# Attention's transposes and value products taken two units at a time, from the fifth query tile on

## The chip, the cores and the metric

The kernel runs on one core of one Trainium2 chip. The metric is the device time of one execution, in microseconds (us), of which the median over several runs is taken. TensorE does the matmuls and the transposes, VectorE and ScalarE read their results out of PSUM, GpSimd scales and splits what lies in SBUF, and SyncE's queue issues the DMAs.

## What is computed

Three stages in a row: causal attention with a decay, a mixture of eight experts whose gates are normalised over rows and columns in turn, and a second feed-forward layer. The change touches the first one only:

```python
B, H, S, D = 2, 8, 576, 64
scores = q @ k.T / sqrt(D) + cum[:, None] - cum[None, :]     # cum: running sum of log f
scores = where(causal, -1e9, scores)
attn = exp(scores - max(scores)); attn /= attn.sum() + 1e-9
out = attn @ v                                               # becomes x of the experts
```

## The kernel before

Attention takes ten query tiles: batch 0 has rows 0, 128, 256, 384 (128 rows each) and 512 (64 rows), batch 1 has row 0 (64 rows) and then 64, 192, 320, 448 (128 rows each). The program counts them `ti` = 0 to 9, so "from the fifth on" is `ti >= 4`. Each tile is four **units** of two heads; unit `pi` = 4 ti + `st`, 40 in all. `nk` is the number of keys that a unit looks at; in the tiles 4 to 9 it is 576, 64, 256, 384, 512 and 576. A 64-row tile puts its two heads into one set of 128 rows.

The schedule is written by hand: every engine executes its instructions in the order in which the program emits them. The main loop has two steps per unit, `s` = 2 pi + a. A step emits, in this order:

- `expo` (line 487): ScalarE's exponential for the step before, with the row sums.
- `normalize` (line 497), where a = 1, for unit pi-1: two small VectorE instructions make 1/sum, and GpSimd multiplies the two heads with it.
- `scores` (line 452; `scores_two`, line 402, for 64-row tiles): two fp32r matmuls per head (L467, L468, or L415) into a PSUM bank of the pool `ps_s`, which has two banks, and VectorE's masked maximum (L480 or L421), which frees the bank. With `nk` = 576 a head takes both banks. The result `p` has three buffers.
- `fill`: one piece (three matmuls, L621 or L640) of expert 0's work, in two lots of 28 pieces, one ready early in the fourth tile, the other once the seventh tile has been attended; in between there are steps without a piece.
- where a = 1: `attend` (line 558) for unit pi-3: the products with v (L567), in column halves of TensorE's array, into one PSUM bank per tile, copied to `xh` and `xl` after the tile's last unit.
- where a = 1: `transposes` (line 516; `transposes_two`, line 436) for unit pi-2: it turns `p` by TensorE (L531 in 64-row halves of the array; L543, L448, L554 with the whole array or a part of its columns) into banks of the pool `ps_t` (three banks), and ScalarE or VectorE copies them to `pT` (two buffers), whichever has the smaller load by the planner's own tally (`evac`, L308 and L312).
- parts of the next tile's preparation: `qs` and `ks` in the steps (st 0, a 0) and (0, 1) split the raw queries and keys into two parts (`hl`, two buffers) on ScalarE, VectorE and GpSimd; `qt_(0)`, `kt_(0)`, `qt_(1)`, `kt_(1)` (`trans`, line 356) in (1, 0), (1, 1), (2, 0) and (2, 1) turn four heads each by TensorE (L360, into `ps_t`), copy them to `qa` or `kt`, and send a DMA that duplicates them to `qb` or `kb`. SyncE's queue also gets the loads of later tiles, of v and of the running sums there.

After the loop follow the gates' last part, the leftover pieces, and the experts.

Of the kernel before, what the change touches and what calls it, by code (L numbers as in the profile page):

```python
# [9 lines left out]
FR = mybir.dt.float32r  # L10
# [6 lines left out]
B, H, S, D = 2, 8, 576, 64  # L17
# [66 lines left out]
def attention_moe_kernel(  # L84
# [44 lines left out]
    with ExitStack() as actx:  # L129
# [8 lines left out]
        ps_s = actx.enter_context(tc.tile_pool(name="ps_s", bufs=2, space=PSUM))  # L138
        ps_t = actx.enter_context(tc.tile_pool(name="ps_t", bufs=3, space=PSUM))
# [193 lines left out]
        def prep(kind, b, i, slots):  # L333

            s0, n = QT[b][i] if kind == "q" else KTL[i]
            st = {}

            def split(half=None):
                if not half:
                    st["raw"] = raws.pop((kind, b, s0))  # L340
                    if (b, i) == (0, 1):
                        o = 1024 * (kind == "k")
                        st["hl"] = big[:, o:o + 1024].rearrange("p (h z d) -> p h z d", z=2, d=D)
                    else:
                        st["hl"] = hlp.tile([128, H, 2, D], FR, tag="hl", name="hl")
                raw, hl = st["raw"], st["hl"]
                hs = slice(0, H) if half is None else slice(4 * half, 4 * half + 4)
                z = 0 if kind == "q" else 1
                hi, lo = hl[:n, hs, z, :], hl[:n, hs, 1 - z, :]
                if half is None:  # L350
                    split2(raw[:n], hi, lo)
                else:
                    nc.scalar.copy(out=hi, in_=raw[:n, hs])
                    nc.vector.tensor_tensor(out=lo, in0=raw[:n, hs], in1=f(hi), op=ALU.subtract)

            def trans(g, early=False):
                hl = st["hl"]
                pt = ps_t.tile([128, 4, 128], FR, tag="pt", name="pt")
                for u in range(4):
                    nc.tensor.transpose(  # L360
                        out=pt[:, u, :n],
                        in_=hl[:n, 4 * g + u].rearrange("p a d -> p (a d)"),
                        identity=idr[:n, :n],
                    )
                hs = slice(4 * g, 4 * g + 4)
                pv = f(pt[:, :, :n])
                if kind == "q":
                    a_, b_ = qa[slots[g]], qb[slots[g]]
                    if n == 64:
                        evac(quads(a_)[:, :, 0:4:3], pv.rearrange("p (u z) t -> p u z t", z=2), 4 * n, 0.125)  # L370
                    else:
                        evac(a_[:, :, :n], pv, 4 * n, 0.125)
                    if early:
                        evac(b_[0:64, :, :n], pv[0:64], 4 * n, 0.125)
                    else:
                        duplicate(b_[0:64], a_[0:64])
                        if g:
                            cum_q(b, i, g, slots[g])
                else:
                    o = kbase[b] + s0  # L380
                    evac(kt[:, hs, o:o + n], pv, 4 * n)
                    if early:
                        evac(kb[0:64, hs, o:o + n], pv[64:128], 4 * n)
                    else:
                        duplicate(kb[0:64, hs, o:o + n], kt[64:128, hs, o:o + n])

            return split, trans
# [170 lines left out]
        def attend(u):  # L558
            n, nk, h, b, pT = u["n"], u["nk"], u["h"], u["b"], u["pT"]
            if h == 0:  # L560
                u["tile"]["x"] = ps_x.tile([128, 4, 128], F32, tag="x", name="x")
            x = u["tile"]["x"]
            nblk = (nk + 127) // 128
            for j in range(nblk):
                w = 128 if j == 4 else min(128, nk - 128 * j)
                for a in range(2):
                    nc.tensor.matmul(  # L567
                        out=x[64 * a:64 * a + 64, h // 2, :n], lhsT=vts[b, j][:w, h + a, :],
                        rhs=pT[:w, 128 * j + 64 * a:128 * j + 64 * a + 64] if n == 64 else pT[:w, a, j * n:(j + 1) * n],
                        start=j == 0, stop=j == nblk - 1,  # L570
                    )
            if h == H - 2:
                c, t0 = divmod(b * S + u["s0"], CH)
                nc.scalar.copy(out=xh[c][:, :, t0:t0 + n], in_=x[:, :, :n])
                nc.vector.tensor_tensor(
                    out=xl[c][:, :, t0:t0 + n], in0=x[:, :, :n], in1=f(xh[c][:, :, t0:t0 + n]), op=ALU.subtract
                )
                spent("act", 90 + 3.4 * n)
                spent("dve", 90 + 4.2 * n)
# [80 lines left out]
        units = []  # L660
# [14 lines left out]
        def make_preps(ti):  # L675
            b, i = tiles[ti]
            slots = [(2 * ti) % 3, (2 * ti + 1) % 3]
            return prep("q", b, i, slots), prep("k", b, i, slots)
# [20 lines left out]
        wtasks = [lambda i=i: wsplit(i) for i in range(8)]  # L699
        gates, logits, ready = [], [], []  # L700
        nu = len(units)
        for s in range(2 * nu + 8):
            pi, a = divmod(s, 2)
            ti, st = divmod(pi, 4)
            live = pi < nu
            prepping = live and ti + 1 < len(tiles)
            if prepping and st == 0 and a == 0:
                (qs, qt_), (ks, kt_) = make_preps(ti + 1)
            if 1 <= s <= 2 * nu:
                expo(units[(s - 1) // 2], (s - 1) % 2)  # L710
            if a and 1 <= pi <= nu:
                normalize(units[pi - 1])
            if live:
                scores(units[pi], a)
            if s < 16:
                warm((2,2,2,2,2,2,2,2,1,1,1,1,1,1,1,1)[s])
            elif s in (17,19,21,25,27):
                warm_late(1)
            fill()
            fills += ready  # L720
            ready = []
            if a and 3 <= pi < nu + 3:
                w = units[pi - 3]
                attend(w)
                if w["h"] == H - 2 and w["ti"] in (2, 6, 9):
                    c = (2, 6, 9).index(w["ti"])
                    gates.append(c)
                    if c < 2:
                        ready.append(filler(c))
                elif gates:  # L730
                    logits.append(gate(gates.pop(0)))
            elif logits:
                gate_end(*logits.pop(0))
            if a and 2 <= pi < nu + 2:
                transposes(units[pi - 2])
            if first:
                first.pop(0)()
            if prepping:
                nb_, ni = tiles[ti + 1]
                if (st, a) == (0, 0):  # L740
                    if ti == 3:
                        pad(2)
                    elif ti == 4:
                        pad(1)
                    elif ti in (5, 6):
                        unpad(0 if ti == 5 else 2)
                    cum_q(nb_, ni, 0, (2 * ti + 2) % 3)
                    qs()
                elif (st, a) == (0, 1):
                    ks()  # L750
                    if ti:
                        next_loads(ti + 2)
                elif (st, a) == (1, 0):
                    qt_(0)
                elif (st, a) == (1, 1):
                    if ti == 3:
                        pad(0)
                    elif ti == 5:
                        unpad(1)
                    kt_(0)  # L760
                    load_v(nb_, ni)
                elif (st, a) == (2, 0):
                    qt_(1)
                elif (st, a) == (2, 1):
                    kt_(1)
            if late_rows and s >= 2:
                late_rows.pop(0)()
            if a:
                continue
            s = pi  # L770
            if s == 3:
                nc.gpsimd.tensor_copy(out=wgc[:, :, 0, :], in_=wg)
                nc.gpsimd.tensor_tensor(out=wgc[:, :, 1, :], in0=wg, in1=f(wgc[:, :, 0, :]), op=ALU.subtract)
            if s == 7:
                wts.load(0, 0, stage)
                wts.load(0, 1, stage)
            if s == 8:
                cum_k(1, 0, 256)
            if s == 22:
                cum_k(1, 256, 576)  # L780
            if s >= 12 and wtasks:
                wtasks.pop(0)()
# [1101 lines left out]
```

## Time and profile before

| | us |
|---|---|
| median of 3 runs | 1094.24 (1094.22 to 1094.34) |
| profiled execution, span from the first to the last instruction | 1097.7 |
| TensorE busy in the span | 1090.1 |
| VectorE busy | 839.7 |
| ScalarE busy | 541.6 |
| GpSimd busy, all of it in the first 165 us | 75.3 |

The profiled execution has no time of its own beside its span. TensorE's busy time is of little use here: the ends of matmuls are modelled and overlap, so that a stretch of 5 us reads 5.00 even where an instruction began late. What is read instead is the distance from one TensorE instruction's start to the next one's. Attention's loop takes about the first 163 us; the paired part of the change would begin at some 60 us.

### The profile page before, as it was taken

The page shows a single profiled execution, that of the slowest core. Times are in us where ns is not written, and L with a number is a line of the kernel's source. Part 1 is how long each engine was busy: PE and PEld are TensorE (multiplying, and loading weights), DVE is VectorE, ACT ScalarE, POOL GpSimd, SP SyncE. Part 2 cuts the span into 40 slices and gives each one's busy share as a digit, 9 for nine tenths or more (in the row PEclk, how much of TensorE's full clock was granted, in tenths as well). Part 3 has the DMA queues.
Part 4 walks back from the last instruction along what each step waited for, and adds up shares of the span by engine and source line. Part 5 has one row for each costly group of instructions (what it writes and reads, how often), then busy time and mean ns, then how long its engine had stood idle before and what let it go on. Part 6 is the DMA issues. An engine that isn't in the chain of part 4 may idle for free.

```text
span 1097.7 us, 18374 instructions
## 1 busy us (share of the span) xinstructions
PE 1090.1 (99%) x6838; PEld 970.0 (88%) x6838; DVE 839.7 (76%) x1891; ACT 541.6 (49%) x1287; POOL 75.3 (7%) x124
## 2 busy tenths in 40 slices
PE   9999999999999999999999999999999999999998
PEld 8788778988989899898989989898898989899997
DVE  7755646878797887977888796888877559778994
ACT  7756642354435252443524335252443448877881
POOL 6534420000000000000000000000000000000000
PEclk9799999999999999999999999999999999999999
DMA  6534302022342424325243343424323341261502
GB/s 147 134 78 108 87 11 87 1 89 78 123 135 77 144 83 149 121 87 158 91 151 98 127 137 109 153 85 147 102 100 96 106 162 42 76 202 51 171 1 87
DMA packets 103805, 114.98 MB, mean 105 GB/s; under 512 B 35236, under 2 KB 63860, under 8 KB 103716
## 3 DMA queue, kind: packets, MB, share of 16 engines
q1 hardware_dynamic: 103716, 113.81, 33.6%
q8 instruction: 54, 0.88, 0.3%
q14 instruction: 35, 0.29, 0.1%
HBM read 82.24 MB, written 27.07 MB: 100 GB/s over the span
## 4 chain that ended last, share of the span: by engine, by line
PE 98%; DVE 1%; ACT 1%; issue 0%; POOL 0%; DVEq 0%; POOLq 0%
PE bank L855 33%; PE bank L1265 29%; PE bank L1737 9%; PE bank L1647 4%; PE ph L825 3%; PE x L567 3%; PE bank L1576 2%; PE spare L1647 2%; PE pa L855 2%; PE pa L640 2%; PE ph L621 1%; PE sp L467 1%; PE pt L360 1%; PE pt L531 1%; PE wt L394 1%; PE sp L468 1%
## 5 line engine op out<-in xcount | busy, mean ns | idle before, releaser
L855 PE MATMUL bank<-w2h,big 128*128 128x512 f32 x924 | 300.2, 394 | 0.0
L855 PEld LDWEIGHTS bank<-w2h,big 128*128 128x128 f32 x924 | 173.8, 188 | 38.7 <-DVE hid_b L833 0.2
L855 PE MATMUL bank<-w2l,big 128*128 128x512 f32 x528 | 207.5, 393 | 0.0
L1294 ACT COPY snap<-bank 128x288 f32<-128x288 f32 x168 | 66.6, 396 | 175.2 <-PE bank L1265 174.8
L855 PEld LDWEIGHTS bank<-w2l,big 128*128 128x128 f32 x528 | 99.3, 188 | 20.9
L832 ACT ACTIVATE big<-c 128x288 fp32r<-128x288 f32 x168 | 74.9, 446 | 83.7 <-DVE c L1299 79.7
L833 DVE SCALAR_TENSOR_TENSOR big<-c,big 128x288 fp32r<-128x288 f32 x140 | 64.0, 457 | 57.1 <-ACT big L832 54.5
L1030 DVE SCALAR_TENSOR_TENSOR acc<-bank,P,acc 128x512 f32<-128x512 f32 x132 | 92.3, 744 | 18.8 <-PE bank L855 18.8
L1265 PE MATMUL bank<-tt,ss 128*128 128x288 f32 x672 | 103.2, 295 | 0.0
L1265 PE MATMUL bank<-xh,ss 128*128 128x288 f32 x448 | 103.1, 295 | 0.0
L1265 PEld LDWEIGHTS bank<-tt,ss 128*128 128x128 f32 x672 | 93.9, 188 | 0.0
L1299 DVE TENSOR_TENSOR c<-bank,snap 128x288 f32<-128x288 f32 x168 | 75.8, 451 | 20.1 <-PE bank L1265 19.7
L1011 ACT CAST hb<-da 128x512 fp32r<-128x512 f32 x38 | 23.7, 624 | 107.4 <-DVE da L986 96.0
L1265 PEld LDWEIGHTS bank<-xh,ss 128*128 128x128 f32 x448 | 76.6, 188 | 0.0
L1265 PE MATMUL bank<-xl,ss 128*128 128x288 f32 x224 | 66.5, 297 | 0.0
L1265 PE MATMUL bank<-xh,w1l 128*128 128x288 f32 x224 | 66.2, 296 | 0.0
L1265 PE MATMUL bank<-xl,w1h 128*128 128x288 f32 x224 | 66.2, 295 | 0.0
L1265 PE MATMUL bank<-xh,w1h 128*128 128x288 f32 x224 | 66.1, 295 | 0.0
L75 DVE TENSOR_TENSOR w2l<-stg,w2h 128x512 fp32r<-128x512 f32 x60 | 41.2, 689 | 14.6 <-ACT w2h L74 14.1
L855 PE MATMUL bank<-w2h,hid_b 128*128 128x512 f32 x132 | 51.7, 391 | 0.0
L511 POOL TENSOR_SCALAR p<-p,rs 128x256 f32<-128x256 f32 (+5 forms) x72 | 42.0, 595 | 68.7 <-DVE rs L507 47.5
L1265 PE MATMUL bank<-tt,w1h 128*128 128x288 f32 x224 | 46.3, 295 | 0.0
(314 smaller groups left out, 2467.4 us busy)
## 6 DMA issues: line engine op xcount, KB each, us to landing
stg<-in_moe_w_dram SPq DMA_DIRECT2D x64, 512.0 KB
wb<-w_in_b SPq DMA_DIRECT2D x42, 256.0 KB
raw<-in_moe_w_in_dram SPq DMA_DIRECT2D x16, 512.0 KB
raw<-in_moe_w_out_dram SPq DMA_DIRECT2D x16, 512.0 KB
w_in_b<-hb SPq DMA_DIRECT2D x18, 256.0 KB
w_out_h<-hb SPq DMA_DIRECT2D x16, 256.0 KB
w_out_l<-da SPq DMA_DIRECT2D x16, 256.0 KB
w_in_f<-da SPq DMA_DIRECT2D x12, 256.0 KB
```

What stands on the lines that cost most here:

```text
L75: (lo_engine or nc.vector).tensor_tensor(out=lo, in0=raw, in1=f(hi), op=ALU.subtract)
L511: nc.gpsimd.tensor_scalar(out=p[:n, a, :nk], in0=p[:n, a, :nk], scalar1=r[:n, a:a + 1], scalar2=1.0, op0=ALU.mult, op1=ALU.mult,)
L567: nc.tensor.matmul(out=x[64 * a:64 * a + 64, h // 2, :n], lhsT=vts[b, j][:w, h + a, :], rhs=pT[:w, 128 * j + 64 * a:128 * j + 64 * a + 64] ...
L832: nc.scalar.activation(out=hh, in_=ph, func=AF.Relu)
L833: nc.vector.scalar_tensor_tensor(out=hl, in0=ph, scalar=0.0, in1=f(hh), op0=ALU.max, op1=ALU.subtract)
L855: nc.tensor.matmul(out=pa, lhsT=a_[:, ts_], rhs=w[wn][ft_], start=(first and n == 0), stop=(last and n == 2),)
L1030: nc.vector.scalar_tensor_tensor(out=acc[t], in0=pa, scalar=P[:, t, e:e + 1], in1=acc[t], op0=ALU.mult, op1=ALU.add)
L1265: nc.tensor.matmul(out=by_chunk(out_) if len(v_.shape) == 3 else out_, lhsT=u, rhs=v_, start=first and m == 0, stop=m == 5, skip_group_che ...
L1294: nc.scalar.copy(out=t, in_=bank["x", g])
L1299: nc.vector.tensor_tensor(out=t, in0=bank[of, g], in1=snap[with_, g], op=ALU.add)
L1647: nc.tensor.matmul(out=out_, lhsT=a_(kk, pa), rhs=b_(kk, pb), start=first and q == 0, stop=q == 5, skip_group_check=True,)
L1737: nc.tensor.matmul(out=bk[b][:, cs], lhsT=a_[:, ts_], rhs=w[wn][i][:, cs], start=i == 0 and q == 0, stop=i == 3 and q == 2,)
```

## The change

From unit 16 on (`ti >= 4`) attend and transposes are no longer emitted for one unit at the end of each odd step, but for two units at once, at the very start of the first step of every odd unit (`pi` odd, a = 0). Such a group emits, where there is a next tile, `qt_(st // 2)` with its result in a bank of the scores' pool `ps_s`, and `kt_(st // 2)`; then transposes of unit pi-3, attend of pi-5 and pi-4, transposes of pi-2. The splits `qs` and `ks` of a tile move from the steps (0, 0) and (0, 1) of the tile before it to (3, 0) and (3, 1) of the tile before that. The gate's part is asked for in the same steps as before.

```diff
-            def trans(g, early=False):
+            def trans(g, early=False, bank=None):
                 hl = st["hl"]
-                pt = ps_t.tile([128, 4, 128], FR, tag="pt", name="pt")
+                pool, tag = bank or (ps_t, "pt")
+                pt = pool.tile([128, 4, 128], FR, tag=tag, name="pt")
...
+        PAIRED = 4
+        turned = attended = 0
+
+        def turn_to(n):
+            nonlocal turned
+            todo = [lambda u=u: transposes(u) for u in units[turned:max(turned, min(n, nu))]]
+            turned += len(todo)
+            return todo
+
+        def attend_to(n):
+            nonlocal attended
+            todo = units[attended:max(attended, min(n, nu))]
+            attended += len(todo)
+            return todo
...
+        def pair_group(pi, turns):
+            for t in turns:
+                t()
+            todo = turn_to(pi - 1)
+            for t in todo[:1]:
+                t()
+            for w in attend_to(pi - 3):
+                attend_unit(w)
+            for t in todo[1:]:
+                t()
+
+        ahead = {}
         for s in range(2 * nu + 8):
...
+            paired = ti >= PAIRED
             prepping = live and ti + 1 < len(tiles)
             if prepping and st == 0 and a == 0:
-                (qs, qt_), (ks, kt_) = make_preps(ti + 1)
+                (qs, qt_), (ks, kt_) = ahead.pop(ti + 1, None) or make_preps(ti + 1)
+            if paired and pi % 2 and a == 0:
+                turns = [lambda: qt_(st // 2, bank=(ps_s, "s")), lambda: kt_(st // 2)] if prepping else []
+                pair_group(pi, turns)
...
-            if a and 3 <= pi < nu + 3:
-                w = units[pi - 3]
-                attend(w)
...
+            if not paired and a:
+                for w in attend_to(pi - 2):
+                    attend_unit(w)
...
-            if a and 2 <= pi < nu + 2:
-                transposes(units[pi - 2])
+            if not paired and a:
+                for t in turn_to(pi - 1):
+                    t()
...
-                    qs()
+                    if ti < PAIRED:
+                        qs()
                 elif (st, a) == (0, 1):
-                    ks()
+                    if ti < PAIRED:
+                        ks()
...
-                    qt_(0)
+                    if not paired:
+                        qt_(0)
...
+                elif ti + 1 >= PAIRED and ti + 2 < len(tiles):
+                    if a == 0:
+                        ahead[ti + 2] = make_preps(ti + 2)
+                    ahead[ti + 2][a][0]()
```

## Rows read from the trace of the kernel before

**Rows 1.** Page, part 4: the chain that ended last, by engine.

```profile
PE 98%; DVE 1%; ACT 1%; issue 0%; POOL 0%; DVEq 0%; POOLq 0%
```

**Rows 2.** TensorE in order of time: start, length, line, matmul, count; one unit.

```profile
121.40 0.45 PE L360 MATMUL pt<-idr,hl 128*128 128x128 f32 x4
121.69 0.46 PE L467 MATMUL sp<-kt,qa 128*128 128x512 f32 x1
121.99 0.40 PE L468 MATMUL sp<-kb,qb 96*128 96x512 f32 x1
122.23 0.34 PE L621 MATMUL ph<-xh,big 128*128 128x384 f32 x1
122.40 0.33 PE L621 MATMUL ph<-xl,big 128*128 128x384 f32 x1
122.57 0.34 PE L621 MATMUL ph<-xh,big 128*128 128x384 f32 x1
122.84 0.88 PE L567 MATMUL x<-pT,v 128*64 128x128 f32 x12
123.65 0.59 PE L531 MATMUL pt<-idn,p 64*128 64x64 f32 x12
124.04 0.48 PE L360 MATMUL pt<-idr,hl 64*128 64x64 f32 x4
124.45 0.50 PE L467 MATMUL sp<-kt,qa 128*128 128x512 f32 x1
124.79 0.40 PE L468 MATMUL sp<-kb,qb 96*128 96x512 f32 x1
```

**Rows 3.** TensorE in order of time: a visit two units later, without preparation.

```profile
130.91 1.09 PE L567 MATMUL x<-pT,v 128*64 128x128 f32 x16
131.94 0.71 PE L531 MATMUL pt<-idn,p 64*128 64x64 f32 x16
132.58 0.40 PE L467 MATMUL sp<-kt,qa 128*128 128x288 f32 x1
```

**Rows 4.** TensorE in order of time: unit 37's second scores, 576 keys.

```profile
138.64 0.29 PE L468 MATMUL sp<-kb,qb 96*128 96x288 f32 x1
139.07 0.40 PE L467 MATMUL sp<-kt,qa 128*128 128x288 f32 x1
139.31 0.30 PE L468 MATMUL sp<-kb,qb 96*128 96x288 f32 x1
```

**Rows 5.** VectorE in order of time: the reduction under which Rows 4 stood.

```profile
138.49 0.52 DVE L480 CUSTOM_DVE_ANT_0 p<-sp,mask,nmax 128x288 f32<-128x288 f32 x1
```

**Rows 6.** Groups by line, 20 to 165 us: count, then busy us, mean ns.

```profile
L480 DVE CUSTOM_DVE_ANT_0 p<-sp,mask 128x384 f32<-128x384 f32 x16 | 8.7, 544 | 3.4 <-PE sp L468 2.0 <-POOL p L511 1.4
...
L308 ACT COPY pT<-pt 128x512 f32<-128x512 f32 x30 | 16.9, 587 | 29.1 <-PE pt L531 20.1 <-PE pt L543 5.0 <-PE pt L448 3.4
```

**Rows 7.** All engines in order of time: unit 33's second head, scores to scaling.

```profile
123.19 0.67 DVE L480 CUSTOM_DVE_ANT_0 p<-sp,mask 128x512 f32<-128x512 f32 x1
...
124.96 0.74 ACT L492 ACTIVATE p<-p,nmax 128x512 f32<-128x512 f32 x1
...
126.65 0.15 DVE L503 TENSOR_SCALAR rs<-sums 128x6 f32<-128x6 f32 x1
...
127.19 1.36 POOL L511 TENSOR_SCALAR p<-p,rs 128x512 f32<-128x512 f32 x2 [1.90 <-DVE rs L507]
```

**Rows 8.** Windows of 5 us: busy us (instructions) by engine, granted clock, DMA share, GB/s.

```profile
40.00:45.00 5.00, 4.05 (x40) 2.95 (x38) 4.49 (x11) 3.95 (x10) 3.76 (x4) 0.88 0.37 84
45.00:50.00 5.00, 5.00 (x34) 3.24 (x32) 3.52 (x11) 2.78 (x9) 2.33 (x6) 0.50 0.62 158
...
55.00:60.00 5.00, 5.00 (x44) 3.40 (x43) 2.25 (x7) 0.83 (x3) 1.86 (x4) 0.76 0.42 122
...
105.00:110.00 5.00, 5.00 (x45) 4.14 (x45) 3.49 (x11) 2.94 (x8) 4.32 (x6) 1.00 0.21 46
```

**Rows 9.** TensorE in order of time: products with v inside the half-clock stretch.

```profile
49.82 1.55 PE L567 MATMUL x<-pT,v 128*64 128x128 f32 x12
```

More of the change, by code (lines that the diff above doesn't have):

```diff
@@ L701, in attention_moe_kernel, with attend_unit @@
         nu = len(units)
+        PAIRED = 4
[10 more added lines that the diff above has]
+            return todo
+        def attend_unit(w):
+            attend(w)
+            if w["h"] == H - 2 and w["ti"] in (2, 6, 9):
+                c = (2, 6, 9).index(w["ti"])
+                gates.append(c)
+                if c < 2:
+                    ready.append(filler(c))
+        def pair_group(pi, turns):
[9 more added lines that the diff above has]
+        ahead = {}
         for s in range(2 * nu + 8):
@@ L721, in attention_moe_kernel @@
             ready = []
-            if a and 3 <= pi < nu + 3:
-                w = units[pi - 3]
-                attend(w)
[L725 to L732, printed above, removed]
+            if not paired and a:
+                for w in attend_to(pi - 2):
+                    attend_unit(w)
+            if a and gates and (paired or units[max(0, pi - 3)]["h"] != H - 2):
+                logits.append(gate(gates.pop(0)))
+            if not a and logits:
                 gate_end(*logits.pop(0))
-            if a and 2 <= pi < nu + 2:
-                transposes(units[pi - 2])
+            if not paired and a:
+                for t in turn_to(pi - 1):
+                    t()
             if first:
@@ L759, in attention_moe_kernel @@
                         unpad(1)
-                    kt_(0)
+                    if not paired:
+                        kt_(0)
                     load_v(nb_, ni)
                 elif (st, a) == (2, 0):
-                    qt_(1)
+                    if not paired:
+                        qt_(1)
                 elif (st, a) == (2, 1):
-                    kt_(1)
+                    if not paired:
+                        kt_(1)
+                elif ti + 1 >= PAIRED and ti + 2 < len(tiles):
+                    if a == 0:
+                        ahead[ti + 2] = make_preps(ti + 2)
+                    ahead[ti + 2][a][0]()
             if late_rows and s >= 2:
```

## The prediction, made blind

> **What bounds the kernel now.** I read the chain that ended last first: TensorE holds 98% of it [rows 1], so what counts is the time from one TensorE instruction's start to the next, and every other engine only where TensorE waits for it. Then I read TensorE's order of time through attention, since its busy time doesn't show gaps. Between units 32 and 36 it runs without a wait: the products with v start at 122.84 and again, two units later, at 130.91, so a unit takes 4.03 us [rows 2, 3]. The reader should compare distances of like instructions. Three matmuls of a fill piece start 0.17 us apart (122.23, 122.40, 122.57), but from the last to the first product with v it is 0.27 [rows 2]: 0.10 lost. Twelve products take 0.81 to the next kind of work, sixteen 1.03 [rows 2, 3], so one costs 0.055 and 12 cost 0.66: 0.15 lost on the way out. Twelve 64-row transposes take 0.39 where the next instruction is the keys' transpose of the same shape (123.65 to 124.04), or 0.0325 each; sixteen, 0.52 of work, take 0.64 where scores follow (131.94 to 132.58): 0.12 lost [rows 2, 3]. The first score matmul after transposes then takes 0.34 (124.45 to 124.79) where its like takes 0.24 (121.99 to 122.23): 0.10 lost [rows 2]. A visit to products and transposes thus costs 0.10 + 0.15 + 0.12 + 0.10 = 0.47 us beside its work. After 164 us the list of TensorE's waits is empty as far as I read it (330 us), so what attention saves should reach the end.
>
> **The change, part by part.**
>
> *Fewer visits: -4.6 us.* Two units before: 0.94. A group now enters transposes once (0.10), goes to products (0.12), back (0.15), and out to scores (0.12 + 0.10): 0.59. That saves 0.35. Visits fall from 27 (units 13 to 39) to 14 groups, so 13 x 0.35 = 4.6. The tiles of 64 rows and of 256 keys use other transpose shapes, which I take at the same price; by these rows a saved visit is worth between nothing and 0.47, so this term lies between 0 and 6.1, and I stay at 4.6, as every part of a visit has its own row.
>
> *Queries' and keys' transposes: -2.5 us.* Alone between scores and pieces, the queries' four transposes take 0.29 (121.40 to 121.69), of which 4 x 0.057 (128 columns at the 0.17 per 384 of the pieces) is work, and slow the next matmul to 0.30 from 0.24: 0.12 lost. The keys' four, after transposes, add 0.41 of which 0.13 is work and 0.12 the way out that is paid anyway: some 0.15 lost [rows 2]. In front of the group they stand with other transposes; I charge 0.02 for the changed entry, which leaves 0.25 for each of ten pairs (five tiles, two pairs): 2.5. Bounds: 0 and 2.7.
>
> *Waits that the new order brings: +3.0 us.* Four scores now follow each other with only fill pieces between, where before products and transposes stood after each second one. (a) In the last tile a head needs both score banks. Today the second head's second half starts 0.43 after the matmul before it, where the same pair takes some 0.13 by columns (288 of the 384 that take 0.17), and that matmul takes 0.24 [rows 4]: 0.30 + 0.11 = 0.41, and it goes on when VectorE's 0.52 reduction from 138.49 is through [rows 5]. Units 36 and 38 get the same wait for their first head: 0.8. (b) Between the two lots of fill pieces (units 29 and 30) nothing stands between four scores. By columns each takes 2 x 0.17 = 0.35, so TensorE is through in 1.4, while VectorE needs 0.54 each [rows 6]. The next group's query transposes take a score bank and so wait for the third reduction: 3 x 0.54, a normalisation estimated at 0.3 (twice the 0.15 of its first half [rows 7]) and a hand-over estimated at 0.2 make 2.1 against 1.4. With two slow restarts of 0.11 as in (a) that is 0.9. (c) The second transposes of a group need the bank of the first ones, whose copy waits until the first products have freed `pT`. The copy takes 0.59 on ScalarE [rows 6] plus two hand-overs; the cover is the second products, 0.66 + 0.15 = 0.81 for 12 of them. So 0 to 0.2 a group, more where the splits, now inside the run of four scores, delay VectorE: 0.1 for 13 groups is 1.3. Lower bound of (a) to (c): 0.8; upper: see the rivals.
>
> *Costed at nothing.* The splits of a tile start two steps sooner, so their GpSimd and VectorE work is ready earlier, and stands in GpSimd's queue ahead of scalings; that is in the GpSimd rival. The copies to `qb` and `kb` and the running sums' DMAs go out with their transposes: the first halves a step sooner, the second up to two steps later, for a tile that needs them three units on, some 12 us at 4.03 each [rows 2, 3]. On SyncE's queue the load of the second batch's second v tile waits for unit 19's products, a step later than before; behind it stand loads and copies for tiles that start two or more units on. Units 14 and 15 wait for the first group; nothing but their own `p` buffers hangs on it, and unit 17's scores stand behind that group anyway. If that cover were gone, a late DMA would show as a wait in front of L467. The work after the loop stands behind the same last products with the same pieces between, so nothing of the gain stays there.
>
> *Sum.* -4.6 - 2.5 + 0.8 + 0.9 + 1.3 = -4.1 us: the span would go from 1097.7 to 1093.6. This profiled execution is 3.5 us above the median of the runs; a difference carries over, so the time is 1094.2 - 4.1 = **1090.1 us**.
>
> The Trainium skill, "TensorEngine Tiling (Array Packing)", section Key Properties, says that a change of the tiling mode drains TensorE, and names no other cost of a change of work. By it alone the queries' visit, which keeps the whole array, would lose nothing, where the row shows 0.12. What that would give is the third rival.
>
> **The rivals.**
>
> *Slower: the group's second transposes wait for GpSimd.* Unit pi-2 must be scaled when the group reaches it. Now it has far more time: unit 33's second head has its scores done at 122.23, its transposes start at 131.94 [rows 2, 3], 9.7 later. Then the way from scores to transposes is three pieces (1.5), two scores (0.95) and in the group the queries and keys (0.48), first transposes (0.5), products (1.5): about 5.0. In the trace the chain took from 122.23 to 128.55, 6.3 us: reduction from 123.19, exponential 124.96, sums 126.65, scaling from 127.19 for 1.36 [rows 2, 7]. Against it: most of that is standing behind the copies of transposes that will no longer be there; the four pieces themselves are 0.67 + 0.74 + 0.5 + 1.36 = 3.3. If half of the 1.3 us that are lacking stays, 0.6 in 12 groups is 7.2 us: 1097.3. It decides from 0.34 us a group (no gain). Chance 0.17.
>
> *The clock falls.* From 45 to 55 us the granted clock is 0.50, 1.2 GHz, and the slices on either side are partly so, together 13.6 us [rows 8]; ahead of it TensorE did scores, products and transposes with one wait and without pieces. The stretch without pieces at 105 to 110 us stays at 1.00 today [rows 8], but the change puts transposes and the waits of (b) together there. Twelve products take 1.55 at the half clock against 0.88 [rows 2, 9], so another 13.6 us would cost 13.6 x (1 - 0.88/1.55) = 5.9: 1096.0. Chance 0.10. The Trainium skill, "TensorE: Matmul & The Clock Gate", Part 4, says that transposes don't hold the clock up as matmuls do, which speaks against this change; no run here shows it by itself.
>
> *Only a change of the array's shape costs.* Then a pair of units goes from six such changes (into products, transposes and out, twice) to four, at 0.12 to 0.15 each: 13 x 2 x 0.135 = 3.5 saved, less 3.0 of waits: 1093.7. Against it stands the queries' row. Chance 0.08.
>
> *VectorE takes it all back.* If ten more of the scores in the runs of four wait 0.41 each, the gain is gone: 1094.2. For it: VectorE also carries copies and splits. Against it: with a piece after each score TensorE needs 0.99 per head of 512 keys and VectorE 0.67 plus its share of the rest [rows 2, 7]. Chance 0.07.
>
> **How the numbers follow.** The forecast has 0.58. Less than 0.2% (2.2 us) can't be told from no change by a measurement of this kernel. The forecast's own range is 1087 to 1092: 7.1 of gain less only (a), -6.3, at one end; waits of 5 at the other. It is all faster. The clock, the shape and VectorE rivals end within 0.2%: 0.25; GpSimd slower: 0.17, its time above 1096.4. The range for 8 in 10 takes in the three middle cases and leaves out most of the slower one: below, gains of 4.6 + 2.7 + half of what the first term's upper bound adds (0.7), with no wait but a few tenths, give 1086.5; above, 1096.2.
>
> **What would show it right or wrong.** In the changed kernel's order of TensorE: products of two units start one behind the other 0.66 us apart at 12 products, with no loss between; 14 visits from unit 14 on; queries', keys' and `p`'s transposes in one run. Unit 36's and 38's first heads start late behind VectorE; so do scores or queries' transposes near 107 us. Wrong would be: GpSimd's scaling ending just ahead of a group's second transposes (the slower rival), a clock below 1.00 after 60 us, waits on VectorE in front of most third and fourth scores, or a first score after the group that is slower than 0.34.

## The result, and the profile after

The changed kernel takes 1100.22 us (median of 6 runs, 1099.34 to 1104.35) against 1094.29 for the kernel before: a ratio of 1.0054, 95% interval 1.0037 to 1.0071. It is slower, by 5.9 us by the medians and 4.0 to 7.8 by the interval, where 4.1 us of gain was forecast. The changed kernel's longer executions spend more time below the full clock: three at a mean granted clock of 1.000 took 1099.34 to 1099.38 us, the one at 0.994 took 1104.35. Its profiled execution took 1101.71 us with a span of 1100.0; lines above L356 keep their numbers, those of the loop's helpers are one higher (L361 is the former L360, L468 the former L467).

The two profiled executions differ ahead of the change too: the half-clock stretch of [rows 8] (13.6 us) lasts 3.4 us in the one after. So everything below is counted from unit 16's first score matmul to the experts' first matmul. That **stretch** is 108.00 us before (59.70 to 167.70) and 113.33 after (55.49 to 168.82): 5.3 us more, close to the difference of the medians. What is lost is lost here. Behind the stretch the profiled execution of the changed kernel takes 931.2 us and that of the kernel before 930.0; the sixteen kernels below take 929.4 to 930.2 there, among them e4 and e7, which differ from the changed kernel by their splits alone, so this 1.2 us is not put down to the change.

Where TensorE waits in this stretch, after; each row has the line that waits, what it waits for, us in total, how often, the longest:

```profile
PE pt L361 <- POOL hl L320: 3.6, 4, 1.4
PE sp L468 <- DVE nmax L481: 2.3, 4, 0.8
PE pt L361 <- DVE rs L504: 0.6, 1, 0.6
PE sp L416 <- DVE nmax L422: 0.2, 1, 0.2
PE pt L532 <- POOL p L512: 0.2, 1, 0.2
PE g L585 <- DVE nmax L481: 0.2, 1, 0.2
```

Before, the same view has one row, 0.3 us on a reduction. Summed from the waits that the order of time shows on TensorE's rows, the stretch holds 7.19 us of waiting after and 0.31 before: 6.9 more. Without them it is 106.14 us against 107.69: 1.6 less. So the saving was small and the waits were large. The first row of the view names the largest of them, the queries' and keys' transposes waiting for a split on GpSimd. All engines in order of time around the first of these, unit 21's group (start, length, engine, line, result, and in brackets the idle time before and who ended it):

```profile
74.49 0.62 ACT L316 CAST hl<-raw 128x512 fp32r<-128x512 f32 x1
74.59 0.42 DVE L318 CAST hl<-raw 128x512 fp32r<-128x512 f32 x1
...
75.15 1.60 POOL L320 TENSOR_TENSOR hl<-raw,hl 128x512 fp32r<-128x512 f32 x1 [5.00 <-PE sp L416]
...
76.73 0.75 POOL L512 TENSOR_SCALAR p<-p,rs 128x576 f32<-128x576 f32 x1
76.81 0.53 PE L361 MATMUL pt<-idr,hl 128*128 128x128 f32 x4 [0.77 <-POOL hl L320]
...
77.44 1.26 POOL L320 TENSOR_TENSOR hl<-raw,hl 128x512 fp32r<-128x512 f32 x1
78.76 0.54 PE L361 MATMUL pt<-idr,hl 128*128 128x128 f32 x4 [1.42 <-POOL hl L320]
```

GpSimd takes the queries' split (1.60), a scaling of `p` (0.75) and the keys' split (1.26) one behind the other, and TensorE starts the queries' transposes right behind the first and the keys' right behind the third. GpSimd had been idle for 5.00 us before: the first split starts when ScalarE's half of it (74.49 for 0.62) is through, so what is late is this chain and not a long queue ahead of it. In the kernel before, the keys' split of the same tile and the transposes that read it:

```profile
82.55 1.29 POOL L320 TENSOR_TENSOR hl<-raw,hl 128x512 fp32r<-128x512 f32 x1
...
85.06 0.54 PE L360 MATMUL pt<-idr,hl 128*128 128x128 f32 x4
```

There the transposes started 1.22 us after their split had ended: products and transposes had stood between. The fronts of the first groups of tiles 6 and 7, after:

```profile
91.33 0.51 PE L361 MATMUL pt<-idr,hl 128*128 128x128 f32 x4 [0.60 <-DVE rs L504]
92.32 0.54 PE L361 MATMUL pt<-idr,hl 128*128 128x128 f32 x4 [0.48 <-POOL hl L320]
...
104.84 0.53 PE L361 MATMUL pt<-idr,hl 128*128 128x128 f32 x4 [0.97 <-POOL hl L320]
```

Counted from start to start, the fronts of the first groups of tiles 5, 6 and 7 lose 5.6 us (0.94 + 1.73, 0.76 + 0.77, 0.14 + 1.26). The 0.76 is not a split's: that split (89.27 for 1.29) had ended at 90.56, and the wait is for VectorE.

The other part is what a group costs where it waits for nothing. TensorE in order of time, the first group of tile 8, against [rows 2] and [rows 3]:

```profile
118.95 0.34 PE L622 MATMUL ph<-xh,big 128*128 128x384 f32 x1
119.13 0.71 PE L361 MATMUL pt<-idr,hl 128*128 128x128 f32 x6
119.61 0.27 PE L532 MATMUL pt<-idn,p 64*128 64x64 f32 x1
119.68 0.24 PE L361 MATMUL pt<-idr,hl 64*128 64x64 f32 x1
119.72 0.25 PE L532 MATMUL pt<-idn,p 64*128 64x64 f32 x1
119.77 0.24 PE L361 MATMUL pt<-idr,hl 64*128 64x64 f32 x1
119.80 0.63 PE L532 MATMUL pt<-idn,p 64*128 64x64 f32 x10
120.36 1.53 PE L568 MATMUL x<-pT,v 128*64 128x128 f32 x24
121.82 0.63 PE L532 MATMUL pt<-idn,p 64*128 64x64 f32 x12
122.39 0.50 PE L468 MATMUL sp<-kt,qa 128*128 128x512 f32 x1
```

The first row of transposes holds the queries' four and two of the keys' (a row shows the shape of its first). The 24 products take 1.46, which is 24 x 0.055 and one way out of 0.14: the two units' products do stand back to back for nothing. But from 119.13 to 122.39 it is 3.26 us, and by [rows 2] the same work in separate visits takes 1.61 + 0.29 + 1.32 (0.81 + 0.39 + 0.12) = 3.22. From start to start nothing is saved; what is saved lies at the edges, where the separate visits lose 0.46 by [rows 2] (two entries into products and two slow first scores at 0.10 each, 0.06 on the matmul behind the queries) and the group 0.11 (0.01 on entry, one first score at 0.10). What eats the saving stands at the front: the first six take 0.48 for 4 x 0.057 + 2 x 0.0325 = 0.29 of work, and the twelve transposes of `p` with the keys' other two take 0.75 until the products where 0.46 of work and 0.12 of way out were due. That is 0.19 + 0.17 = 0.36, where the forecast charged 0.02. Not all of it is the loss of a change of work. The front of tile 5's second group has eight of these transposes of one shape in a row:

```profile
84.73 0.80 PE L361 MATMUL pt<-idr,hl 128*128 128x128 f32 x8
85.36 0.27 PE L449 MATMUL pt<-idn,p 128*64 128x128 f32 x1
```

They take 0.63, or 0.079 each, with no other work between, where the forecast took 0.057 as the work of one. Four of them so lose 0.09 by themselves, and of the 0.19 some 0.10 is left for the change.

The last tile's first group has nothing in front:

```profile
135.58 0.33 PE L622 MATMUL ph<-xh,big 128*128 128x384 f32 x1
135.84 0.71 PE L532 MATMUL pt<-idn,p 64*128 64x64 f32 x16
136.49 1.97 PE L568 MATMUL x<-pT,v 128*64 128x128 f32 x32
138.38 0.71 PE L532 MATMUL pt<-idn,p 64*128 64x64 f32 x16
139.03 0.40 PE L468 MATMUL sp<-kt,qa 128*128 128x288 f32 x1
139.26 0.30 PE L469 MATMUL sp<-kb,qb 96*128 96x288 f32 x1
```

Beside the work it loses 0.09 (into transposes), 0.13, 0.13, 0.13 and 0.10 (the first score): 0.58, where 0.59 was forecast.

Last, scores that wait for their bank, at the first unit of the last tile and in the steps without pieces:

```profile
108.87 0.33 PE L469 MATMUL sp<-kb,qb 96*128 96x384 f32 x1
110.02 0.45 PE L468 MATMUL sp<-kt,qa 128*128 128x384 f32 x1 [0.81 <-DVE nmax L481]
...
132.61 0.29 PE L469 MATMUL sp<-kb,qb 96*128 96x288 f32 x1
133.69 0.40 PE L468 MATMUL sp<-kt,qa 128*128 128x288 f32 x1 [0.79 <-DVE nmax L481]
```

The distances are 1.15 and 1.08 us, where 0.17 and 0.13 would do by columns.

### The profile page after: what moved, and what is told of

It reads as the page before. It is cut to its first block, busy times and chain, and to the rows that moved or that the text cites. A ratio compares the mean times of both kernels' runs of the same rounds, so it can differ in the third digit from the quotient of the medians.

```text
span 1100.0 us, 18359 instructions
## 1 busy us (share of the span) xinstructions
PE 1085.2 (99%) x6838; PEld 968.8 (88%) x6838; DVE 841.2 (76%) x1891; ACT 545.4 (50%) x1287; POOL 74.9 (7%) x124
## 4 chain that ended last, share of the span: by engine, by line
PE 93%; DVE 3%; ACT 1%; POOL 1%; issue 1%; DMA 0%; POOLq 0%; SPq 0%; DVEq 0%; ACTq 0%
PE bank L901 33%; PE bank L1311 28%; PE bank L1783 9%; PE bank L1693 4%; PE ph L871 3%; PE x L568 2%; PE bank L1622 2%; PE spare L1693 2%; PE pa L901 2%; PE pa L641 1%; PE pt L361 1%; PE ph L622 1%; PE pt L532 1%; PE sp L468 1%; PE wt L395 1%
```

## The experiments

In the table "waits" is the sum of the idle time in brackets on TensorE's rows of the stretch, "rest" the stretch without it. The kernel before, run beside them on the same chip, had medians of 1094.36 to 1094.39 us. The ratio is on record with its interval and isn't always that of the medians. The rows marked * hold some TensorE time below the full clock in the stretch, which is in their rest.

| kernel | median us | ratio to before (95%) | stretch | waits | rest |
|---|---|---|---|---|---|
| before | 1094.29 | | 108.00 | 0.31 | 107.69 |
| after | 1100.22 | 1.0054 (1.0037 to 1.0071) | 113.33 | 7.19 | 106.14 |
| e1, preparation behind the group * | 1105.05 | 1.0095 (1.0073 to 1.0117) | 115.49 | 7.15 | 108.34 |
| e2, pairs alone | 1096.84 | 1.0021 (1.0012 to 1.0029) | 110.41 | 4.69 | 105.72 |
| e4, some splits earlier * | 1100.01 | 1.0044 (1.0031 to 1.0057) | 112.63 | 5.84 | 106.79 |
| e6, last two tiles only | 1094.62 | 1.0002 (0.9988 to 1.0016) | 108.01 | 1.28 | 106.73 |
| e7, splits on VectorE | 1096.54 | 1.0027 (1.0013 to 1.0040) | 109.37 | 2.88 | 106.49 |
| e8, products first | 1098.93 | 1.0042 (1.0026 to 1.0058) | 112.76 | 5.74 | 107.02 |
| e14, e7 and e8 | 1098.31 | 1.0029 (1.0012 to 1.0045) | 111.50 | 3.92 | 107.58 |
| e15, e14, last tile single | 1096.03 | 1.0016 (1.0006 to 1.0026) | 109.73 | 2.42 | 107.31 |
| e16, e7, last tile single | 1095.21 | 1.0012 (0.9997 to 1.0026) | 109.22 | 2.26 | 106.96 |
| e17, e7 in tiles 4, 6, 8 only | 1094.48 | 0.9994 (0.9981 to 1.0007) | 107.98 | 1.80 | 106.18 |
| e18, tile 8 only | 1095.10 | 1.0009 (0.9994 to 1.0024) | 108.22 | 1.09 | 107.13 |
| e20, before, splits on VectorE | 1093.65 | 0.9991 (0.9979 to 1.0002) | 107.70 | 0.00 | 107.70 |
| e21, e2, splits on VectorE | 1097.32 | 1.0034 (1.0022 to 1.0046) | 110.96 | 4.62 | 106.34 |
| e22, e21, last tile single | 1097.08 | 1.0016 (1.0000 to 1.0031) | 110.84 | 4.13 | 106.71 |
| e23, keys' transposes in the group * | 1107.32 | 1.0115 (1.0101 to 1.0129) | 122.50 | 12.23 | 110.27 |
| e24, e23, last tile single * | 1109.57 | 1.0137 (1.0123 to 1.0151) | 123.66 | 11.68 | 111.98 |

**e1: the queries' and keys' transposes behind the group.**

```diff
-            for t in turns:
-                t()
...
-            for t in todo[1:]:
+            for t in todo[1:] + turns:
                 t()
```

> The queries' and keys' transposes stand behind each group in place of in front of it; all else as in the changed kernel. Theory (the groups wait for the splits that GpSimd finishes too late, 5.6 us in three groups of the trace): the group's own 2.5 to 3 us now lie ahead of the transposes, the waits on hl vanish, and the time falls from 1099.35 us to about 1094.0 (1093.3 to 1095.0). Rival (the runs of four scores between groups keep VectorE and ScalarE late, whatever the splits do): the waits move to the scores, and the time stays at 1097.5 or more.

The median is 1105.05 us, higher still, but all six executions have a granted clock of 0.989 to 0.998; the profiled one, at 0.998, took 1101.44, as the changed kernel did at 0.998 (1101.05 and 1101.71). So the edit gave nothing back, and more than that isn't shown. That is the rival's time, but the waits did not move to the scores as it had them: the transposes of `p`, now first, wait for GpSimd's scaling instead; in the trace of this kernel, all engines in order of time:

```profile
74.56 1.33 POOL L320 TENSOR_TENSOR hl<-raw,hl 128x512 fp32r<-128x512 f32 x1 [5.04 <-PE sp L416]
...
76.55 0.17 DVE L508 RECIPROCAL rs<-rs 128x2 f32<-128x2 f32 x1
76.88 0.74 POOL L512 TENSOR_SCALAR p<-p,rs 128x576 f32<-128x576 f32 x1 [0.99 <-DVE rs L508]
...
77.68 0.77 PE L449 MATMUL pt<-idn,p 128*128 128x128 f32 x5 [2.24 <-POOL p L512]
```

So the front of the group hides a second wait: `p` isn't ready either. Moving the transposes only changes which chain is late.

**e2: pairs alone, the preparation where it was.**

```diff
-                turns = [lambda: qt_(st // 2, bank=(ps_s, "s")), lambda: kt_(st // 2)] if prepping else []
+                turns = []
...
-                    if ti < PAIRED:
-                        qs()
+                    qs()
```

(and so for `ks`, `qt_`, `kt_`)

> Products with v and transposes of p go in pairs; splits and the queries' and keys' transposes stay in the steps where the kernel before has them. Theory (splits too late): no waits on hl; the fewer visits save up to 4.6 us and the runs of four scores cost 3 to 4, so about 1093.8 (1092.8 to 1095.0). Rival (pairing products and transposes is itself what costs): 1097 or more.

By the medians 3.4 us of the loss go and 2.5 stay; in the stretch 2.9 go and 2.4 stay. The rest is the shortest of all, 105.72: the visits alone save 2.0 us. Of the 4.69 us of waits 3.2 are `p`'s transposes waiting for GpSimd's scaling, 1.7 of them in the tile of 64 keys, whose scores are too short to cover the chain from scores to scaling.

**e4: the splits of tiles 7 to 9 one unit sooner**, two of them into buffers of another pool.

```diff
-                elif ti + 1 >= PAIRED and ti + 2 < len(tiles):
+                if st == (2 if ti > PAIRED else 3) and ti + 1 >= PAIRED and ti + 2 < len(tiles):
```

> As the changed kernel, but the splits for the eighth, ninth and tenth tile start one unit sooner, with buffers of their own for two of these tiles; the seventh tile's splits stay. Theory (splits too late): the waits on hl of some 1.5 us near 91 us and 1.4 us near 104 us go, the 2.6 us near 77 us stay: about 1096.4 (1095.9 to 1097.2). Rival (runs of four scores): the waits move on, 1098.5 or more.

The waits for splits fall from 3.64 to 2.19 us, those of tiles 6 and 7 being gone as expected, but the median doesn't tell it from the changed kernel. The profiled execution has a granted clock of 0.88 and 0.77 from 75 to 85 us, behind the waits of tile 5 that this edit leaves, so this run settles little.

**e7 and e20: the second halves of the second batch's splits on VectorE instead of GpSimd**, in the changed kernel and in the kernel before.

```diff
-                if half is None:
+                if half is None and (b, i) >= (1, 0):
+                    split_w(raw[:n], hi, lo)
+                elif half is None:
                     split2(raw[:n], hi, lo)
```

> As the changed kernel, but the second half of each split for the tiles of batch 1 is done by VectorE (0.69 us each) in place of GpSimd (1.28 us each). Theory A (GpSimd's in-order queue of splits and scalings is too long for the run of scores between two groups): the waits for it in the sixth and eighth tile, 2.4 and 2.0 us above the kernel before, halve: about 1097.0 (1096.2 to 1098.0). Theory B (VectorE is what the run waits for; GpSimd only comes last because it is fed late): no gain, 1099 or more.

> The kernel before, with only the queries' and keys' second halves of the splits of the second batch moved from GpSimd to VectorE; no groups. Theory A (in the changed kernel this edit gave 3.7 us back because GpSimd's splits and scalings stood in the way of transposes that came too soon; in the kernel before, products and transposes between splits and their transposes cover them): 1094.3 us (1093.8 to 1094.8). Rival (GpSimd's splits cost time in any order, so that the edit has nothing to do with the groups): 1092 or less.

In kernels with this edit the lines are two higher again (L363 is the changed kernel's L361). In the changed kernel 3.7 us come back (4.0 in the stretch), as theory A had it, and no row of GpSimd is left among TensorE's waits:

```profile
PE sp L470 <- DVE nmax L483: 1.6, 4, 0.8
PE pt L363 <- DVE rs L506: 0.6, 1, 0.6
PE pt L363 <- DVE nmax L424: 0.5, 1, 0.5
PE sp L418 <- DVE nmax L424: 0.2, 1, 0.2
```

In the order of before the same edit gives 0.7 us by the medians, 0.3 in the stretch, with an interval that takes in no change: a little below what theory A expected, and far from the rival's 2 us. Tile by tile, tiles 4 to 8 are as long as before to 0.01 us, and the 0.3 is a wait for a score bank in the last one that e20 doesn't have. GpSimd's splits cost time only in the new order. The edit does not free GpSimd's queue alone, though. In the changed kernel VectorE's first halves of splits (L318) take 0.42 us where GpSimd does nothing beside them (74.59 and 115.11) and 1.39 and 1.17 where a split of GpSimd's runs (89.45 and 101.58); in e7 the planner's tally gives all of these to ScalarE. How much of the 3.7 us comes by that way no run tells apart. And e7 without any of its waits would still be only 1.5 us shorter than the kernel before (106.49 against 108.00).

**e8, e14, e15: products first, the preparation in the middle**, alone, with e7, and with the last tile ungrouped.

```diff
-            for t in turns:
-                t()
             todo = turn_to(pi - 1)
-            for t in todo[:1]:
-                t()
             for w in attend_to(pi - 3):
                 attend_unit(w)
-            for t in todo[1:]:
+            for t in todo[:1] + turns + todo[1:]:
                 t()
```

> As the changed kernel, but a group begins with the two units' products, which wait for nothing, then the first unit's transposes, the queries' and keys', the second unit's. Everything that waited gets 1.3 to 2.0 us more. Theories A and B both: the waits at the front of the groups in the sixth and eighth tile go for the most part, 1096.3 (1095.3 to 1097.3). Theory C (what a group waits for is set off by the group before, so that a wait only moves): 1098.5 or more.

> Both edits together: products first, and the splits' second half on VectorE. Theory A: only the last tile's waits for score banks are left, 1095.0 (1094.2 to 1096.0). Theory B: as products first alone or slower, 1096.3 or more.

> As the one before, but the last tile goes unit by unit again. The last tile and the tail are 1.2 us longer in the changed kernel than before, by waits for score banks; that goes, and the tail's saving of 1.3 us with it. Theory A: 1094.3 (1093.4 to 1095.3), no more than the kernel before. Theory B: 1096 or more.

All three times lie where the rivals had them. In e8, tiles 5 and 7 gain 1.2 us each by the later transposes, but tile 8 loses 0.6 and the last tile with the tail 1.4, and new waits of 1.7 us come up: the second transposes for ScalarE's copy of the first ones, which nothing covers once the products stand ahead of both. In the trace of e8:

```profile
136.50 0.71 PE L532 MATMUL pt<-idn,p 64*128 64x64 f32 x15 [0.67 <-ACT pT L308]
...
146.61 0.89 PE L532 MATMUL pt<-idn,p 64*128 64x64 f32 x16 [0.45 <-ACT pT L308]
```

This is wait (c) of the forecast, absent where products stand between the two. With e7's splits (e14) this order is behind e7 itself, by the medians and by 2.1 us in the stretch; the intervals overlap.

**e6, e18, e16, e17: which tiles are grouped.** e6 sets `PAIRED = 8`; the others change the test, and the conditions of the gate and the splits to match, e16 and e17 with e7's splits:

```diff
-            paired = ti >= PAIRED
+            paired = PAIRED <= ti < 9        # e16, PAIRED = 4
+            paired = ti in PAIRED            # e17: (4, 6, 8); e18: (8,)
```

> As the changed kernel, but pairs begin at the ninth tile, so that four groups and the tail remain of 14 groups. Theory (splits too late): no group is left that waited for hl; the visits saved (some 2.0 us) stand against the last tile's waits for score banks (1.5 us): about 1093.9 (1093.0 to 1095.0). Rival (every pair costs about the same, 5.1 us over 14 groups): 1096 or more.

> The changed kernel with groups in the ninth tile alone, the splits as they were. The run with groups in the last two tiles took 1094.6, with 1.04 us less in the ninth and 1.06 more behind it. Theory A: the 1.06 behind it is the last tile's own waits on its score banks, so here the ninth keeps 1.0: 1093.4 us (1092.9 to 1093.9). Rival (the time goes over to the tile behind): 1094.3 (1094.0 to 1094.7).

> The changed kernel with the queries' and keys' second halves of the splits on VectorE (as in the earlier run of that edit, which took 1096.5 us) and with the last tile's visits after each unit again. Theory A (GpSimd's queue, plus the last tile's waits on its two score banks): the last two tiles cost about 1.0 more than they must when the last is grouped, but the run with groups in the last two tiles alone showed the grouped tile 8 handing 1.0 to the tile behind it; so 0.5 to 1.9 less: 1094.6 us (1093.8 to 1095.6), no better than before. Rival (what is left, 2.2 us, is spread over all groups): 1096.0 or more.

> The same VectorE splits, and groups only in the tiles that make no splits in a short lead or end in the last scores: the fifth, seventh and ninth. Theory A: each grouped tile keeps its saved visits (two each, 0.35 apiece, 2.1 us in three tiles), and the grouped tile costs about 1 us of waits where it is the fifth (a short tile): 1093.5 us (1092.6 to 1094.6). Rival (a grouped tile only hands its time to the next one, since VectorE and ScalarE are the real limit of a tile): 1094.3 or a little above.

None of the four can be told from the kernel before (e16 lies at its edge). e6 had tile 8 shorter by 1.04 us and the rest longer by 1.06, which I read as a gain there and waits behind it; e18 was to keep the gain and didn't. The reading was wrong: at a tile's border the groups leave the products four units behind where the kernel before is three behind, so one unit's products (1.03 in [rows 3]) pass over the border, and the 1.04 were mostly work put off: when the last tile's first score starts, TensorE has done 336 products in e6 and e18 and 352 in the kernel before. e18 also shows the wait at unit 36 with the last tile ungrouped (distance 1.08, as in the changed kernel): so it goes with the run of four scores that the group of tile 8 leaves behind, and not with the last tile's own groups.

**e21, e22: pairs alone with e7's splits**, and the same with the last tile ungrouped (the edits of e2, e7 and e16 together).

> Only products and p's transposes are paired; queries' and keys' transposes, and the splits in front of them, stand where the kernel before has them; the second halves of the second batch's splits are on VectorE. Theory B (the saving was priced too high, beside the waits): in the run with pairs alone, the stretch from unit 16's first scores to the experts spent 4.7 us waiting against 0.3 before, and 106.0 us otherwise other than 107.7, so the visits saved about 2 us and not 4.6. Here most of the 3.2 us on GpSimd should be gone and the 1.3 on VectorE's reductions stay: a stretch of 107.0 to 107.8 us, 1093.6 us (1093.0 to 1094.4). Rival C (the forecast's 4.6 is right, and restarts behind the waits hid it): a stretch of 105.5, 1092.0 us or less.

> As the run before it, with the last tile's visits after each unit again. With all transposes in the groups this edit was worth 1.3 us. Theory B: less here, as the ninth tile's last group still puts four scores in front of VectorE: 1093.3 us (1092.4 to 1094.2), with one wait of about 0.8 us on VectorE at unit 36. Rival C: 1091.5 us or less.

Both theories missed: 1097.32 and 1097.08 us, and the 3.3 us of waits for scalings are all still there. In the trace of e21 around tile 5:

```profile
75.39 0.69 DVE L328 TENSOR_TENSOR big<-stg,big 128x512 fp32r<-128x512 f32 x1
...
75.99 0.15 DVE L506 TENSOR_SCALAR rs<-sums 128x6 f32<-128x6 f32 x1
76.18 0.17 DVE L510 RECIPROCAL rs<-rs 128x2 f32<-128x2 f32 x1
...
76.54 0.74 POOL L514 TENSOR_SCALAR p<-p,rs 128x576 f32<-128x576 f32 x1 [6.57 <-DVE nmax L424]
...
77.34 0.77 PE L451 MATMUL pt<-idn,p 128*128 128x128 f32 x5 [0.96 <-POOL p L514]
```

GpSimd had been idle for 6.57 us. The scaling is late since its 1/sum stands on VectorE behind a split of expert weights. So GpSimd's splits explain the changed kernel (e7), not the pairs alone: there the way from scores to scaled `p` is too long for the short tile. That is read from the rows; no run moved the split of the weights. The rest, 106.34, again has visits worth 1.4 us, not 4.6.

**e23, e24: the keys' transposes in the group, the queries' where they were**, the splits in their old steps and their second halves on VectorE. Against e21 (e22 for e24):

```diff
-                turns = []
+                turns = [lambda: kt_(st // 2)] if prepping else []
```

> Products and p's transposes paired, with the keys' transposes in front of each group and the queries' alone between scores as before; splits in their old steps, their second halves on VectorE. Theory B says that the front of a group with both kinds costs 0.3 to 0.5 us beside its work, most of it at the change from the queries' 128-row transposes to 64-row ones; keys' alone then stand in front for nothing, and this run is 0.5 to 1.0 us shorter than the one with pairs alone: 1092.9 us (1092.2 to 1093.8). Rival (any transposes in front cost about what they cost alone, or the keys' split comes too late for a group one step sooner): 1093.6 us or more, with waits of the keys' transposes on VectorE.

> As the run before it, with the last tile's visits after each unit again: 0.3 us less than it, 1092.6 us (1091.8 to 1093.6), by theory B the best of these orders. Rival: no better than the kernel before with its splits on VectorE, 1093.6 us.

Slower by 13 and 15 us. The keys' transposes now come a step sooner than before, their splits don't, and TensorE stands still for them:

```profile
PE pt L363 <- DVE hl L328: 10.0, 5, 2.9
```

So the theory on the front could not be tried in this way; what the run shows is how little lead there was: one step sooner costs 10 us in five waits, although a split is only 0.60 us on ScalarE (at 79.40) and 0.69 on VectorE (at 80.07).

## Why the prediction was wrong

The miss is 9.4 us in the stretch (-4.1 forecast, +5.3 measured), and it divides by the table: 3.9 in waits (6.9 more, where (a) to (c) made 3.0) and 5.5 in the rest (-1.6, where -4.6 and -2.5 made -7.1).

- **The step that failed first is "Costed at nothing"**: that the splits "start two steps sooner, so their GpSimd and VectorE work is ready earlier". A step isn't a time. The transposes moved as well, and the work that had stood between split and transposes, the visits of odd steps, moved behind them into the group. GpSimd's two splits of 1.3 us with a scaling between them had about 1 us to spare before (0.7 to 1.5 between a split's end and its transposes in tiles 5 to 8) and none after. e7 with e20 shows it: 3.7 us come back when these splits leave GpSimd, against 0.7 in the order of before. In the stretch the waits for splits, `rs` and `p` are 4.45 us, none of which was in the sum.
- **The term of the queries' and keys' transposes, -2.5, was worth nothing.** e2 and the changed kernel differ by where the preparation stands, and so do e21 and e7: moved into the groups, it makes the rest longer by 0.42 and 0.15 us. The forecast took 0.057 or 0.0325 us as a transpose's work and the remainder of its time for the loss of a change that a new place would save. But eight in a row with no change among them take 0.079 each (84.73), so the 0.06 that the queries' four lose inside their 0.29 goes wherever they stand. In seven fronts that wait for nothing (at 58.60, 67.97, 84.73, 97.17, 110.49, 119.13 and 126.78) they lose 0.17 to 0.63 us beside the forecast's work, 0.37 on average, where 0.02 was charged. The 0.27 of their old places is tile 8's; in tile 4 of the kernel before (66.15 and 69.43) the same count gives some 0.5.
- **Fewer visits, -4.6:** 14 groups as forecast, products back to back, and 0.58 against 0.59 in a group with nothing in front. But over all groups e2 and e21, which have no fronts, save 2.0 and 1.4 us in the rest. Why is open. The price was read in the long tiles and carried over to the short ones, but that isn't all: e6, with six groups in place of eleven visits in the last two tiles, saves 0.96 in the rest, where 5 x 0.35 would be 1.75. Slow restarts behind waits are in these numbers and weren't told apart.
- **The waits on score banks,** (a) and (b), were seen in the right places and sized 1.7. What the scores of the last tile lose beside their columns is 2.90 us from start to start, against 1.68 before: 1.2 more, where (a) had 0.8. At 110.02 it is 0.98, where (b) had 0.9; the hand-over of 0.2 in (b) is in no row, and behind GpSimd's first split (75.15 for 1.60) TensorE starts 0.06 us later, at 76.81. (c), 1.3, did not come while products stand between, and did in e8 when they didn't.
- **The rivals.** The slower one named the right engine and the wrong instruction: scalings cost 0.2 us in the changed kernel, splits 3.6; scalings do wait in e1, e2 and e21. VectorE takes its part (the 2.3 and 0.6 above). The clock rival did not occur: granted 1.00 from 60 us on in the changed kernel's profiled execution. "Only a change of the array's shape costs" is right in part: the queries' 0.12, which spoke against it, is half in the transposes themselves, and at 119.61, where 128-row transposes give way to 64-row ones, some 0.10 us goes. But the other 0.17 of that front has no such change. The Trainium skill, "TensorEngine Tiling (Array Packing)", section Key Properties, has a change of the tiling mode drain TensorE; the 0.10 at 119.61 agrees with it.

No order among these runs beats the kernel before beyond its interval. The best is the kernel before with e7's splits (e20, 0.9991, 0.9979 to 1.0002), which has no groups. The lower end of the forecast's range, 1087, is 0.9 below what its own -6.3 gives; the result lies far above the other end.

## What to carry to other kernels

When an instruction and its consumer are both moved, count in the trace the time between the producer's end and the consumer's start, and what stands between them in every in-order queue; here about 1 us of slack was used up by moving what had filled it. Before time is put down to a change of work, look for a run of the same instructions without a change: eight transposes in a row took 0.079 us each here, where 0.057 had been taken for their work and the remainder for a loss that could be saved. And in a schedule in which one engine has next to no waits (0.3 us in 108), batching its work may open some: every kernel with groups here has 1.1 to 12.2 us of them. As I read it, the work between small visits is the time in which the others keep up.

## What the runs showed of the hardware that was not expected

The granted clock fell behind waits of TensorE, but not behind each, and their length doesn't tell which. In e23, three of the five waits for splits, of 2.13, 2.87 and 1.94 us (ending at 59.92, 80.81 and 125.80), stand at a window with a mean of 0.66; two of 1.31 and 1.76 do not. In e24, with waits of nearly the same lengths, the one of 1.77 has such a window and the one of 1.95 has none; in e1 the clock stays at 1.00 behind 2.24 us at 77.68 and falls behind 1.33 at 92.95 (0.89 and 0.77 from 90 to 100 us). Windows of e23 in 5 us: busy us by engine, then the granted clock, DMA share and GB/s.

```profile
75.00:80.00 5.00, 2.94 (x20) 2.62 (x18) 3.25 (x13) 3.72 (x10) 1.05 (x2) 1.00 0.00 1
80.00:85.00 5.00, 4.19 (x52) 3.75 (x53) 1.05 (x3) 1.18 (x3) 1.03 (x1) 0.66 0.60 131
85.00:90.00 5.00, 5.00 (x53) 4.76 (x53) 2.47 (x11) 2.85 (x8) 0.88 (x3) 1.00 0.13 30
```

So a wait can cost more than its own length: part of the time runs at the lower of the two levels, 1.2 GHz, afterwards. The changed kernel's waits, up to 1.42 us, had no such fall in its profiled execution; the same two waits of tile 5 had one in e4 (0.88 and 0.77 from 75 to 85 us).

VectorE's cast of a half of a split took 0.41 to 0.54 us with no split of GpSimd's running beside it, and 0.91 to 1.39 with one, in the kernel before and in the changed one alike.
